# Output tiles of 128 columns and stores of 256, 128 and 126 rows in an FFT filter with a gated feed-forward block

## The chip, the core and the metric

The kernel runs on one core of a Trainium2 chip. TensorE (PE in the profile) multiplies matrices; its weight loads are listed apart as PEld. VectorE (DVE), ScalarE (ACT) and GpSimd (POOL) do the elementwise work. SyncE (SP) issues almost all DMAs, one after the other, from one queue of instructions; the transfers themselves run on 16 DMA engines that all queues of the core share. The metric is the device time of one execution in microseconds (us), and it is compared with the median of several executions.

## The reference

The input `x` has 8 sequences of 3136 tokens with 256 channels. Each channel is filtered in the frequency domain, and the result goes through a gated feed-forward block:

```python
X = np.fft.rfft(x, axis=1)
y = np.fft.irfft(X * (filt_r + 1j * filt_i)[None], n=x.shape[1], axis=1)

h = np.maximum(y @ w_in, 0.0)                       # 256 -> 1024
hp = pad(h, one zero token on either side)
conv_out = sum(conv_w[k] * hp[:, k:k + S, :] for k in range(3))
return (h / (1 + np.exp(-conv_out)) @ w_out)        # 1024 -> 256
```

The output has the shape of the input, 8 x 3136 x 256 in fp32, that is 25.7 MB.

## The kernel before

The Fourier transform is written as matrix products in four stages, each over 14 pairs of columns (`NP = 14`) of one sequence: stage 1 multiplies `x` with a table and stores to `a_dram`; stage 2 loads from `a_dram`, multiplies with a small table and applies the filter on DVE and POOL; stage 3 multiplies with a table and stores to `b_dram`; stage 4 loads from `b_dram` and leaves the filtered sequence in SBUF as two fp32r halves, `yh` and `yl` (a high part and the rest, so that products are made as three matmuls each). The first sequence is transformed ahead of the main loop. The transforms of the other seven are spread over the main loop: stages 2, 3 and 4 are 98 pieces there and stage 1 is 94, since four of them are done ahead of the loop. A stage-1, stage-2 or stage-3 piece is 2 to 4 matmul records (`L231`, `L235`) on a PSUM bank `ps_t`, a stage-4 piece is 8 (`L255`). A stage can start only when all 14 pieces of the stage before are stored.

The feed-forward block treats the eight sequences as one line of 25,095 positions (one zero token between two of them) and cuts it in 50 units of `UO = 510` positions. A unit needs eight steps, one for each block of 128 hidden channels, which makes 400 steps; the last eight, of unit 49, have only 105 positions. Step `m` is written out in this order (the order in the program is the order on each engine, a manual schedule): `evacuate` of the step seven back, the second half of the transform pieces of step `m - 1` (`from_bank`: a store to `a_dram` or `b_dram`, or the filter), new loads, the first half of the pieces of step `m` (`transform`), then `inner` (6 matmuls of 512 columns into a PSUM bank `ps_h`), `relu` and `centre` (ACT), the taps of the convolution (DVE), `sigmoid` (ACT), `gate` (DVE), `round_g` (ACT, the high half of the gated values), `rest_g` (POOL, the low half), and `project` of the step six back. Each batch of transforms is planned over 48 steps, which are six units.

`project` multiplies the gated values with `w_out`. The gated values `g` (128 hidden channels x 510 positions) are the stationary operand, cut in four tiles of 128, 128, 127 and 127 columns; each tile takes three matmuls of 256 columns. Two tiles share one of two PSUM banks, so the first bank `po0` holds 256 output rows and the second, `po1`, holds 254. After the last of the eight steps `evacuate` copies each bank to an SBUF tile `ot` (DVE, `L522`) and SP stores it: one DMA of 256 rows, written as 2 x 128 partitions, and one of 254 rows, written as 2 x 127 partitions (`L527`); a row is 1 KB. Only where a zero token falls into a bank is it stored in up to two pieces for each tile (`L533`, `L535`). Before unit 42 other DMAs follow these stores on SP: loads, tables, filters and stores of the transforms.

The values of the convolution (`t`) and the gated values (`g0`, `g1`) rotate through pools of four buffers each, 510 values, which is 2040 bytes in each partition.

DMAs issued by SP rotate over eight semaphores. Each waits first for the DMA that had the semaphore before it, and the queue behind it waits with it.

Of the kernel before, what the change touches and what calls it, by code (L numbers as in the profile page):

```python
# [9 lines left out]
F32 = mybir.dt.float32  # L10
F32R = mybir.dt.float32r
# [5 lines left out]
S = 3136  # L17
# [3 lines left out]
D = 256  # L21
# [3 lines left out]
UO = 510  # L25
ROW = S + 1
# [96 lines left out]
def tile_fft_filter_gated_ffn(  # L123
# [16 lines left out]
    nc = tc.nc  # L140
    B = x.shape[0]

    def hi_act(dst, src):
        nc.scalar.activation(dst, src, AF.Copy)  # L144
# [4 lines left out]
    def lo_pool(dst, src, hi):  # L149
        nc.gpsimd.tensor_tensor(out=dst, in0=src, in1=hi.bitcast(F32), op=ALU.subtract)  # L150
# [111 lines left out]
    with (  # L262
# [4 lines left out]
        raws, ws, fts, tabs, rows, zs, pss = {}, {}, {}, {}, {}, {}, {}  # L267
# [154 lines left out]
    wp = ctx.enter_context(tc.tile_pool(name="wp", bufs=2, reuse_waits="tile"))  # L422
# [4 lines left out]
    outf = out.rearrange("b s d -> (b s) d")  # L427
    LEN = B * ROW - 1
    NU = -(-LEN // UO)
    ts, hs, gs, pos, joined = {}, {}, {}, {}, {}  # L430

    def at(m):

        return (m // NF, m % NF) if 0 <= m < NF * NU else None

    def place(u):

        b, tok = divmod(UO * u, ROW)
        return b, tok, min(UO, LEN - UO * u)
# [30 lines left out]

    def centre(u, f):
        n = place(u)[2]
        ts[u, f] = t = wp.tile([128, UO], F32, name="t", bufs=4)[:, 0:n]
        nc.scalar.activation(t, hs[u, f][:, 1:n + 1], AF.Copy, scale=cw[:, 1, f:f + 1])  # L474

    def tap(u, f, k):
# [7 lines left out]
        nc.vector.tensor_mul(ts[u, f], hs.pop((u, f))[:, 1:place(u)[2] + 1], ts[u, f])  # L484

    def round_g(u, f):
        gs[u, f] = [wp.tile([128, UO], F32R, name=f"g{h}", bufs=4)[:, 0:place(u)[2]] for h in range(2)]
        hi_act(gs[u, f][0], ts[u, f])

    def rest_g(u, f):  # L490
        lo_pool(gs[u, f][1], ts.pop((u, f)), gs[u, f][0])

    def tiles_of(u):

        n = place(u)[2]
        if n <= 128:
            return [(0, n)]
        assert n == UO
        return [(0, 128), (128, 128), (256, 127), (383, 127)]

    def project(u, f):
        gh, gl = gs.pop((u, f))
        if f == 0:
            pos[u] = [ps_o.tile([128, 512], F32, name=f"po{k}") for k in range(2)]
        for t, (c, n) in enumerate(tiles_of(u)):
            o = pos[u][t // 2][0:n, t % 2 * D:t % 2 * D + D]
            first, last = f == 0 and t % 2 == 0, f == NF - 1
            nc.tensor.matmul(o, lhsT=gh[:, c:c + n], rhs=wo[0][:, f], start=first, stop=False, skip_group_check=True)  # L508
            nc.tensor.matmul(o, lhsT=gh[:, c:c + n], rhs=wo[1][:, f], start=False, stop=False, skip_group_check=True)  # L509
            nc.tensor.matmul(o, lhsT=gl[:, c:c + n], rhs=wo[0][:, f], start=False, stop=last, skip_group_check=True)  # L510

    def evacuate(u, f):
        if f < NF - 1:
            return
        tiles = tiles_of(u)
        for k in range(2):
            part = tiles[2 * k:2 * k + 2]
            if not part:
                continue
            n = part[0][1]  # L520
            ot = wp.tile([128, 2, D], F32, name="ot", bufs=3)[0:n, 0:len(part)]
            nc.vector.tensor_copy(ot.rearrange("p t d -> p (t d)"), pos[u][k][0:n, 0:len(part) * D])  # L522
            p = UO * u + part[0][0]
            b, tok = divmod(p, ROW)
            if tok + len(part) * n <= S:
                rows = outf[p - b:p - b + len(part) * n].rearrange("(t p) d -> p t d", p=n)
                nc.sync.dma_start(out=rows, in_=ot)  # L527
                continue
            for t in range(len(part)):
                b, tok = divmod(p + t * n, ROW)  # L530
                r, end = p + t * n - b, min(n, S - tok)
                if end > 0:
                    nc.sync.dma_start(out=outf[r:r + end], in_=ot[0:end, t])  # L533
                if end + 1 < n:
                    nc.sync.dma_start(out=outf[r + end:r + n - 1], in_=ot[end + 1:n, t])  # L535

    NW = 6 * NF
    plan, tails, heads = {}, {}, {}
# [102 lines left out]
    with tc.manual_schedule(engines=COMPUTE | {mybir.EngineType.SP}):  # L641
# [4 lines left out]
        for m in range(NF * NU + PLAG + 1):  # L646
            p1, p2, p3, p4, p6, p7 = (at(m - k) for k in (1, 2, 3, 4, PLAG, PLAG + 1))
            new, old = plan.get(m, []), plan.get(m - 1, [])
            if p7:
                evacuate(*p7)  # L650
# [11 lines left out]
            if p1:  # L662
                relu(*p1)
                centre(*p1)
# [4 lines left out]
            if p3:  # L669
                round_g(*p3)  # L670
# [3 lines left out]
            if p4:  # L674
                rest_g(*p4)
# [49 lines left out]
```

## Time and profile before

| | us |
|---|---|
| median of three runs | 1828.39 |
| lowest and highest | 1823.7 and 1836.49 |
| the profiled execution | 1834.37 |
| its span, first to last instruction | 1832.4 |
| DVE, ACT, POOL busy | 1182.3, 1151.3, 817.0 |
| first matmul of the main loop | 119.7 |

The profile has one row for each group of instructions: the line of the kernel, the engine, the operation, the tile written and those read. Records of matmuls overlap, as they are pipelined: 0.28 us in a row of the timeline is not the pace, which is the distance of two starts. The chain of work that ended last goes back from the last instruction to what released it; its rows have a start, a length and the instruction or the transfer, and are lengths along the chain. In the timeline of SP a row is a DMA instruction and its length is the time that SP's sequencer needed to issue it; the transfer comes after it. The table of stretches lists for each stretch its length, the busy time of the engines asked for with the number of instructions, the granted clock of TensorE, the mean share of the 16 DMA engines that is busy, and GB/s.

### The profile page before, as it was taken

What the parts mean: (1) busy time and instruction counts of PE and PEld (TensorE: products, weight loads), DVE (VectorE), ACT (ScalarE), POOL (GpSimd) and SP (SyncE); (2) the same over time, 40 slices, a digit from 0 to 9 for tenths busy, and PEclk for the clock granted to TensorE, in tenths of its full rate; (3) what the DMA queues carried; (4) which work ended last, traced back from release to release, by engine and by line L of the source; (5) the groups of instructions that cost most, each with busy time, mean ns of one, the idle gap of its engine ahead of it and who ended that gap; (6) DMA issues with size and microseconds to landing.
All of it is one profiled execution on the core that took longest, in us unless ns stands there. A gap on an engine that the chain in (4) does not pass through costs nothing.

```text
span 1832.4 us, 26781 instructions
## 1 busy us (share of the span) xinstructions
PE 1625.3 (89%) x9384; PEld 1402.4 (77%) x9384; DVE 1182.3 (65%) x1810; ACT 1151.3 (63%) x1989; POOL 817.0 (45%) x695
## 2 busy tenths in 40 slices
PE   6889879888898888988889899897998799999997
PEld 5778668777787677877778677886878678989997
DVE  6757655566655665666666667665765578767775
ACT  3376456655676556755478555774666656778885
POOL 3514435433453334634346334553445444564443
PEclk8899899999999999999999999998999899999999
DMA  9635543354524545245542464326542254310000
GB/s 273 200 111 175 184 145 104 117 166 139 160 69 123 162 138 159 65 129 158 161 141 71 132 207 144 107 67 183 177 139 85 66 158 140 109 35 25 25 24 28
DMA packets 159016, 229.16 MB, mean 125 GB/s; under 512 B 14970, under 2 KB 108002, under 8 KB 158882
## 3 DMA queue, kind: packets, MB, share of 16 engines
q1 hardware_dynamic: 157922, 226.53, 41.0%
q8 instruction: 75, 1.23, 0.3%
q10 hardware_dynamic: 960, 0.92, 0.2%
q14 instruction: 59, 0.48, 0.1%
HBM read 156.74 MB, written 70.65 MB: 124 GB/s over the span
## 4 chain that ended last, share of the span: by engine, by line
PE 60%; DMA 20%; issue 9%; POOL 4%; ACT 4%; DVE 2%; SPq 1%; POOLq 0%; ACTq 0%; DVEq 0%
PE ps_h L175 8%; PE ps_h L176 8%; PE ps_h L177 8%; DMA tin<-b_dram 7%; PE po L508 7%; PE po L509 7%; PE po L510 7%; PE ps_t L231 7%; DMA a_dram<-st 5%; PE ps_t L255 4%; PE ps_t L235 4%; POOL g L150 3%; DMA tab<-in_s 2%; DMA tab<-in_i 1%; DMA tin<-a_dram 1%
## 5 line engine op out<-in xcount | busy, mean ns | idle before, releaser
L478 DVE SCALAR_TENSOR_TENSOR t<-ps_h,cw,t 128x510 f32<-128x510 f32 (+1 forms) x800 | 588.5, 736 | 420.9 <-ACT t L474 418.1
L150 POOL TENSOR_TENSOR g<-t,g 128x510 fp32r<-128x510 f32 (+1 forms) x400 | 503.9, 1268 | 238.3 <-ACT g L144 215.1
L469 ACT ACTIVATE ps_h<-ps_h 128x512 f32<-128x512 f32 (+1 forms) x400 | 233.0, 583 | 364.6 <-PE ps_h L177 364.4
L508 PE MATMUL po<-wo,g 128*128 128x256 f32 (+2 forms) x1576 | 451.7, 287 | 0.7 <-DVE ot L522 0.5
L509 PE MATMUL po<-wo,g 128*128 128x256 f32 (+2 forms) x1576 | 450.1, 286 | 0.0
L510 PE MATMUL po<-wo,g 128*128 128x256 f32 (+2 forms) x1576 | 445.8, 283 | 0.0
L247 POOL TENSOR_TENSOR z<-z,v 120x512 f32<-120x512 f32 x112 | 147.3, 1315 | 552.6 <-DVE v L246 405.1
L474 ACT ACTIVATE t<-ps_h,cw 128x510 f32<-128x510 f32 (+1 forms) x400 | 272.3, 681 | 130.0 <-POOL g L150 96.1
L175 PE MATMUL ps_h<-y,wi 128*128 128x512 f32 (+1 forms) x688 | 338.5, 492 | 0.0
L508 PEld LDWEIGHTS po<-wo,g 128*128 128x128 f32 (+2 forms) x1576 | 304.1, 193 | 19.9 <-ACT t L474 1.5
L509 PEld LDWEIGHTS po<-wo,g 128*128 128x128 f32 (+2 forms) x1576 | 303.2, 192 | 17.9
L510 PEld LDWEIGHTS po<-wo,g 128*128 128x128 f32 (+2 forms) x1576 | 303.4, 192 | 0.6 <-POOL g L150 0.5
L176 PE MATMUL ps_h<-y,wi 128*128 128x512 f32 (+1 forms) x688 | 278.6, 405 | 0.3 <-DVE y L147 0.3
L177 PE MATMUL ps_h<-y,wi 128*128 128x512 f32 (+1 forms) x688 | 278.7, 405 | 0.0
L484 DVE TENSOR_TENSOR t<-ps_h,t 128x510 f32<-128x510 f32 (+1 forms) x400 | 268.5, 671 | 0.9 <-ACT t L481 0.8
L144 ACT ACTIVATE g<-t 128x510 fp32r<-128x510 f32 (+1 forms) x400 | 245.2, 613 | 4.4 <-PE po L509 4.0
L481 ACT ACTIVATE t<-t 128x510 f32<-128x510 f32 (+1 forms) x400 | 245.4, 613 | 2.1 <-DVE t L478 2.0
L150 POOL TENSOR_TENSOR y<-z,y 128x448 fp32r<-128x448 f32 x98 | 136.8, 1404 | 171.6 <-ACT y L144 171.6
L226 ACT ACTIVATE st<-ps_t 112x512 f32<-112x512 f32 x192 | 113.5, 594 | 98.6 <-DMA b_dram<-st 63.6
L175 PEld LDWEIGHTS ps_h<-y,wi 128*128 128x128 f32 x688 | 136.0, 198 | 39.0 <-issue 18.0
L176 PEld LDWEIGHTS ps_h<-y,wi 128*128 128x128 f32 x688 | 136.4, 198 | 38.0 <-issue 18.6
L177 PEld LDWEIGHTS ps_h<-y,wi 128*128 128x128 f32 x688 | 135.0, 196 | 31.8
(80 smaller groups left out, 1713.6 us busy)
## 6 DMA issues: line engine op xcount, KB each, us to landing
filt<-in_filt SPq DMA_DIRECT2D x98, 512.0 KB
tin<-a_dram SPq DMA_DIRECT2D x98, 224.0 KB
b_dram<-st SPq DMA_DIRECT2D x98, 224.0 KB
tin<-b_dram SPq DMA_DIRECT2D x98, 224.0 KB
tin<-in_x SPq DMA_DIRECT2D x94, 224.0 KB
a_dram<-st SPq DMA_DIRECT2D x94, 224.0 KB
out<-ot SPq DMA_DIRECT2D x46, 254.0 KB
out<-ot SPq DMA_DIRECT2D x45, 256.0 KB
```

The source lines that it names most:

```text
L144: nc.scalar.activation(dst, src, AF.Copy)
L150: nc.gpsimd.tensor_tensor(out=dst, in0=src, in1=hi.bitcast(F32), op=ALU.subtract)
L175: nc.tensor.matmul(ps, lhsT=wh, rhs=rh, start=start, stop=False, **kw)
L176: nc.tensor.matmul(ps, lhsT=wh, rhs=rl, start=False, stop=False, **kw)
L177: nc.tensor.matmul(ps, lhsT=wl, rhs=rh, start=False, stop=stop, **kw)
L474: nc.scalar.activation(t, hs[u, f][:, 1:n + 1], AF.Copy, scale=cw[:, 1, f:f + 1])
L478: nc.vector.scalar_tensor_tensor(out=t, in0=h[:, k:place(u)[2] + k], scalar=cw[:, k, f:f + 1], in1=t, op0=ALU.mult, op1=ALU.add)
L481: nc.scalar.activation(ts[u, f], ts[u, f], AF.Sigmoid)
L484: nc.vector.tensor_mul(ts[u, f], hs.pop((u, f))[:, 1:place(u)[2] + 1], ts[u, f])
L508: nc.tensor.matmul(o, lhsT=gh[:, c:c + n], rhs=wo[0][:, f], start=first, stop=False, skip_group_check=True)
L509: nc.tensor.matmul(o, lhsT=gh[:, c:c + n], rhs=wo[1][:, f], start=False, stop=False, skip_group_check=True)
L510: nc.tensor.matmul(o, lhsT=gl[:, c:c + n], rhs=wo[0][:, f], start=False, stop=last, skip_group_check=True)
```

## The change

Three things change. The second bank of a unit is made of tiles of 128 columns too, the last of which reads two columns past the 510 positions; they are set to zero once and never written again, and the two output rows that they give are not stored. The second bank is stored by a DMA of 128 rows and one of 126. And the gated values lie in four fixed pairs of tiles, `ring`, used in turn by `f % 4`; these and the tiles `t` are 576 values long, 2304 bytes, of which 510 are used.

```diff
+    ring = [[wp.tile([128, UO + 66], F32R, name=f"g{i}{h}", bufs=1) for h in range(2)] for i in range(4)]
+    for pair_of in ring:
+        for g in pair_of:
+            nc.gpsimd.memset(g[:, UO:UO + 2].bitcast(F32), 0.0)
...
-        ts[u, f] = t = wp.tile([128, UO], F32, name="t", bufs=4)[:, 0:n]
+        ts[u, f] = t = wp.tile([128, UO + 66], F32, name="t", bufs=4)[:, 0:n]
...
-        gs[u, f] = [wp.tile([128, UO], F32R, name=f"g{h}", bufs=4)[:, 0:place(u)[2]] for h in range(2)]
-        hi_act(gs[u, f][0], ts[u, f])
+        gs[u, f] = ring[f % 4]
+        hi_act(gs[u, f][0][:, 0:place(u)[2]], ts[u, f])
...
-        return [(0, 128), (128, 128), (256, 127), (383, 127)]
+        return [(0, 128), (128, 128), (256, 128), (384, 128)]
...
-            if tok + len(part) * n <= S:
-                rows = outf[p - b:p - b + len(part) * n].rearrange("(t p) d -> p t d", p=n)
+            if k == 0 and len(part) == 2 and tok + 256 <= S:
+                rows = outf[first - b:first - b + 256].rearrange("(t p) d -> p t d", p=128)
                 nc.sync.dma_start(out=rows, in_=ot)
                 continue
-            for t in range(len(part)):
-                b, tok = divmod(p + t * n, ROW)
-                r, end = p + t * n - b, min(n, S - tok)
-                if end > 0:
-                    nc.sync.dma_start(out=outf[r:r + end], in_=ot[0:end, t])
-                if end + 1 < n:
-                    nc.sync.dma_start(out=outf[r + end:r + n - 1], in_=ot[end + 1:n, t])
+            for t, (c, n) in enumerate(part):
+                i, n = 0, min(n, place(u)[2] - c)
+                while i < n:
+                    b, tok = divmod(UO * u + c + i, ROW)
+                    if tok == S:
+                        i += 1
+                        continue
+                    end = min(n, i + S - tok)
+                    if end - i > 16 and (end - i) % 14:
+                        end = i + (end - i) // 16 * 16
+                    r = b * S + tok
+                    nc.sync.dma_start(out=outf[r:r + end - i], in_=ot[i:end, t])
+                    i = end
```

Pieces of the output that are neither of 16 rows or fewer nor a multiple of 14 are cut to a multiple of 16, and the rest follows as a piece of its own.

On the engines this shows at two places. SP's queue at unit 0, within the first batch of transforms, before; a name is the target of the DMA and what it reads, with the shape on the SBUF side, and the numbered DMAHW in brackets is the semaphore whose last DMA is waited for:

```order
133 L590 DMA tab<-in_s 112x224 [waits DMAHW2_49]
134 L527 DMA out<-ot 128x2x256 [waits DMAHW3_49,DVE_49]
135 L527 DMA out<-ot 127x2x256 [waits DMAHW4_49,DVE_49]
136 L227 DMA a_dram_59<-st 112x2x256 [waits DMAHW5_49,Activation_49]
137 L221 DMA tin<-a_dram_58 112x512 [waits DMAHW6_49,PE_49]
```

and now:

```order
133 L601 DMA tab<-in_s 112x224 [waits DMAHW2_49]
134 L532 DMA out<-ot 128x2x256 [waits DMAHW3_49,DVE_49]
135 L545 DMA out<-ot 128x256 [waits DMAHW4_49,DVE_49]
136 L545 DMA out<-ot 126x256 [waits DMAHW5_49]
137 L227 DMA a_dram_59<-st 112x2x256 [waits DMAHW6_49,Activation_49]
138 L221 DMA tin<-a_dram_58 112x512 [waits DMAHW7_49,PE_49]
```

The store of 2 x 127 partitions has become two stores, and everything behind it takes the next semaphore in turn; nothing has changed places.

The end of SP's queue, units 47, 48 and 49, before:

```order
821 L527 DMA out<-ot 128x2x256
822 L527 DMA out<-ot 127x2x256
823 L527 DMA out<-ot 128x2x256
824 L527 DMA out<-ot 127x2x256
825 L527 DMA out<-ot 105x256
```

and now:

```order
873 L532 DMA out<-ot 128x2x256
874 L545 DMA out<-ot 128x256
875 L545 DMA out<-ot 126x256
876 L532 DMA out<-ot 128x2x256
877 L545 DMA out<-ot 128x256
878 L545 DMA out<-ot 126x256
879 L545 DMA out<-ot 96x256
880 L545 DMA out<-ot 9x256
```

The last unit's 105 rows go as 96 and 9. In all SP issues 170 stores of the output where it issued 113. PE, DVE and ACT issue the same instructions in the same order as before, with 128 in the place of 127; POOL has eight small memsets more, ahead of the first step's work.

## What was predicted

> **What bounds the kernel now.** I read the page first, then the chain of waits, then SP's timeline, and last tables of stretches and the waits of PE.
>
> ```profile
> span 1832.4 us, 26781 instructions
> PE 1625.3 (89%) x9384; PEld 1402.4 (77%) x9384; DVE 1182.3 (65%) x1810; ACT 1151.3 (63%) x1989; POOL 817.0 (45%) x695
> ...
> PE 60%; DMA 20%; issue 9%; POOL 4%; ACT 4%; DVE 2%; SPq 1%; POOLq 0%; ACTq 0%; DVEq 0%
> ```
>
> PE is busy for 89%, but only 60% of the chain is PE and 20% is transfers. The full list of the chain shows which: among its longest pieces are 14 loads or stores of the transforms that take 13.5 to 14.5 us each; these are the first and the last.
>
> ```profile
> 298.10 14.31 DMA tin<-b_dram
> ...
> 1607.40 14.21 DMA tin<-b_dram
> ```
>
> SP's timeline shows what stands ahead of them. Two units of one batch:
>
> ```profile
> 558.12 0.99 SPq L527 DMA_DIRECT2D out<-ot  x2
> 559.20 8.21 SPq L227 DMA_DIRECT2D a_dram<-st  x1
> 573.29 0.79 SPq L221 DMA_DIRECT2D tin<-a_dram  x2
> ...
> 595.90 8.14 SPq L227 DMA_DIRECT2D b_dram<-st  x1
> ```
>
> A DMA is issued in 0.3 to 0.5 us, but the one behind a pair of output stores takes 8.2 us, and SP issues nothing meanwhile. Which store does it shows in the table of stretches after the last transform, where the stores of a unit (issued at 1642) are alone (the columns are the length of the stretch, granted clock, DMA share, GB/s):
>
> ```profile
> 1642.00:1644.00 2.00, 1.00 0.40 132
> 1644.00:1646.00 2.00, 1.00 0.06 7
> ...
> 1650.00:1654.00 4.00, 1.00 0.07 24
> ```
>
> After 2 us of spread traffic (the 256 rows) a share of 0.06 to 0.07 stays for ten more: 1 of 16 engines. So the store of 2 x 127 partitions runs on a single DMA engine; what is issued behind it needs that engine too, lands after some 14 us, and is held 8 us in its issue. PE pays for it. One batch of six units, and a stretch after the transforms:
>
> ```profile
> 571.00:796.00 225.00, 198.63 (x1119) 170.62 (x1118) 139.36 (x212) 137.89 (x236) 99.20 (x83) 0.93 0.44 132
> 1640.00:1665.00 25.00, 24.88 (x159) 22.18 (x159) 20.73 (x33) 21.10 (x37) 12.86 (x11) 1.00 0.10 32
> ```
>
> The columns are PE, PEld, DVE, ACT, POOL, granted clock, DMA share, GB/s. In the batch PE is idle for 26.4 us and its clock is 0.93; afterwards it is 99.5% busy at 1.00 and sets the pace. The idle time of PE in that batch, by what ended it:
>
> ```profile
> PE ps_t L255 <- DMA tin<-b_dram: 7.1, 2, 4.4
> PE ps_t L231 <- DMA tab<-in_s: 6.1, 1, 6.1
> PE ps_t L235 <- DMA tin<-a_dram: 5.1, 1, 5.1
> PE ps_t L235 <- issue: 5.0, 1, 5.0
> PE ps_t L231 <- issue: 1.1, 1, 1.1
> PE ps_t L231 <- DMA tab<-in_i: 0.9, 1, 0.9
> PE ps_t L231 <- ACT st L226: 0.7, 1, 0.7
> PE ps_t L255 <- PE ps_t L255: 0.5, 1, 0.5
> ```
>
> The first four, 23.3 us, are loads that were issued behind a blocked SP or ran on the loaded engine; 3.2 us are small.
>
> **What PE needs without these waits.** I price the work at full clock from the chain, where a row ends as the next begins.
>
> ```profile
> 617.31 0.86 PE ps_t L235 x2
> 618.17 0.23 PE ps_h L175
> ...
> 620.99 1.08 PE ps_t L231 x5
> ...
> 629.23 0.86 PE ps_t L231 x4
> ...
> 1627.24 0.88 PE ps_t L255 x8
> ```
>
> A step without transforms is 620.99 - 618.17 = 2.82 us. A piece of stage 2 (`L235`) is 0.86, of stage 1 or 3 (`L231`) 0.86, of stage 4 (`L255`) 0.88. So: 392 steps x 2.82 = 1105.4; stages 1 to 3, (94 + 98 + 98) x 0.86 = 249.4; stage 4, 98 x 0.88 = 86.2. Ahead of the main loop lie 119.7 us (its first matmul), behind the last full step, from 1803.8, 28.6 us:
>
> ```profile
> L175 PE MATMUL ps_h<-y,wi x688: 213/399/1415, 119.7 to 1817.7; 128*128 128x512 f32 x168, 128*128 128x108 f32 x4
> ...
> 1803.67 0.28 PE L510 MATMUL po<-wo,g 128*127 128x256 f32 x1
> 1816.59 9.33 SPq L527 DMA_DIRECT2D out<-ot  x3
> ```
>
> The sum is 1589.3 us, 243 less than the span. That 243 is idle PE and PE at the lower clock after each pause; a batch by the same prices is 48 x 2.82 + 14 x 3.46 = 183.8 us, against 225 measured.
>
> **The change part by part.**
>
> *Stores of 256, 128 and 126 rows.* The 46 stores of 254 rows go. The 128 rows are the first store's form cut in half. For 126 no row shows the spread; bounds: as good as 128 rows (nothing held), or one engine as 127 rows were where a zero token forced them alone:
>
> ```profile
> 1085.92 0.25 SPq L533 DMA_DIRECT2D out<-ot  x1
> 1086.27 2.24 SPq L227 DMA_DIRECT2D a_dram<-st  x1
> ```
>
> There the next issue took 2.24 us, not 8.2. I take the first: the rows show 2 x 128 partitions spread and 2 x 127 not, 127 is a prime, and 126 can be dealt out evenly, as 9 rows for each of 14 engines. "DMA: Bandwidth & Descriptors" of the Trainium skill (section "Why a DMA increments its semaphore by 16 and not by 1") says that a transfer uses the largest number of engines up to 16 that divides its slowest dimension, so 127 gives 1 and 126 gives 14. By that rule the first bound holds; the share of 0.06 agrees with the 1, and no row here shows the 14.
>
> With nothing held, the loads have time: a stage's first load is issued at least two steps of 3 us or more ahead of its use, and the 2 us that the 256 rows took above are the scale of a spread transfer. So the 23.3 us per batch go, and the slow clock behind them, as PE then has no pause longer than 1 us. What is late next are the 3.2 us of small waits: 6.5 batches x 3.2 = 21 us if all stay, 0 if they too came from SP; between ends that near I take the middle, +10.
>
> *57 more issues on SP* (170 stores, not 113), 0.25 to 0.5 us each, 23 us over the run, ahead of the loads in SP's queue. For the copies to `ot` alone SP waits far longer, and with the loads running several pieces ahead this is hidden; I cost it at nothing.
>
> ```profile
> SPq L527 <- DVE ot L522: 338.2, 79, 24.7
> ```
>
> If that cover were gone, 23 us is the end. The semaphores in turn are taken up one place earlier; since no DMA then stays out for 14 us, their waits shrink.
>
> Here a rule speaks against the change. "SBUF — State Buffer" of the Trainium skill (section "The DMA setup-cost knee") gives every transfer a fixed cost of about 2 us and asks for one large transfer, not several. By it 57 more would be an estimated 114 us if nothing hid them, and the sum 1707 us; the trace disagrees for this kernel, whose one large transfer is the one that blocks.
>
> *The end.* The last store of 105 rows is issued behind a 254-row store: three issues, with their waits, take 9.33 us from 1816.59 to 1825.9, and the landing lasts to the end at 1832.4, 6.5 us more. Behind spread stores the landing is some 2 us, like the 256 rows above, which is -4.5, and part of the issue is hold: -6 us, with 0 and -8 as ends.
>
> *128 columns for 127.* The loads of weights on PE by shape:
>
> ```profile
> L508 PEld LDWEIGHTS po<-wo,g 128*128 128x128 f32 x784 | 153.6, 196 | 19.6 <-ACT t L474 1.5
> ...
> L508 PEld LDWEIGHTS po<-wo,g 128*127 128x127 f32 x784 | 149.1, 190 | 0.0
> ```
>
> A load is 6 ns longer, but overlaps its neighbours, and the matmul streams 256 columns either way: 0. Bounds: 2352 x 6 ns = +14 us if it lies on the path, and as much below if mixed widths cost something now. The copies to `ot` have one more partition, no more elements in each: 0.
>
> *Fixed tiles, 2304 bytes apart.* The same four-deep turn, and the same waits on PE, DVE and ACT; eight memsets on POOL are under 1 us, hidden by the first steps. Whether the distance changes a pace no row shows; 0, with the 14 us above as its bound either way.
>
> **Sum.** 1589.3 - 6 + 10 = 1593 us of span. The profiled execution has 2.0 us around its span (1834.4) and is 0.33% above the median of the runs, 1828.4; so 1595 x 0.9967 = 1590 us.
>
> **The rivals.**
>
> *126 rows run on one engine too, so the change does half of what it says.* By the row above a quarter of the hold stays (2.24 for 8.2), by the bytes half of the transfer (126 of 254 KB). The gain of 243 - 6 shrinks by a quarter to a half, 59 to 118 us; some 1680. For it: no row shows 126. Against: 127 is the one odd number here.
>
> *ACT becomes the bound in stage 4.* With PE's pauses gone nothing lets ACT catch up.
>
> ```profile
> L474 ACT ACTIVATE t<-ps_h,cw 128x510 f32<-128x510 f32 x392 | 269.5, 687 | 129.2 <-POOL g L150 96.1 <-ACT ps_h L469 1.1
> L481 ACT ACTIVATE t<-t 128x510 f32<-128x510 f32 x392 | 243.1, 620 | 1.6 <-DVE t L478 1.6
> L144 ACT ACTIVATE g<-t 128x510 fp32r<-128x510 f32 x392 | 242.9, 620 | 2.2 <-PE po L509 1.9
> L469 ACT ACTIVATE ps_h<-ps_h 128x512 f32<-128x512 f32 x392 | 231.0, 589 | 362.8 <-PE ps_h L177 362.6
> ...
> L144 ACT ACTIVATE y<-z 128x448 fp32r<-128x448 f32 x98 | 102.0, 1075 | 1.7 <-DVE z L630 1.7
> ```
>
> A step with one stage-4 piece is 3.59 us on ACT and 2.82 + 0.88 = 3.70 on PE. If gaps between ACT's instructions and the stores of stage 1 make it 4.0, 98 steps lose 0.3 each: +30 us, 1620. Over a whole batch ACT's 137.9 us are well under 183.8, so it is a loss of that stage alone.
>
> *SP's issues are on the path after all*, so that every further transfer costs its 0.4 us: 57 x 0.4 = +23, 1613. For it: the queue is in order, and loads stand behind the stores. Against: the 338 us above.
>
> *Slower.* The 4704 matmuls of `project` read their weights from tiles at another distance, and PE is the bound: if that or the full width stretched each by 52 ns, the gain of 243 is lost. The nearest row is the 6 ns above, so I see no reason for so much.
>
> **How the numbers follow.** Chances: my forecast, within 1565 to 1615, 0.73; ACT, 1610 to 1650, 0.11; SP's issues, 1605 to 1650, 0.04; 126 rows on one engine, 1650 to 1710, 0.06; below 1565, where widths and small waits all fall my way, 0.03; no gain or a loss by PE's weights, 0.03. The predicted time is the first's, 1590. The range from 1562 to 1650 holds the first three and leaves out about 0.12. A measurement of this kernel can tell about 1% from no change: faster by more 0.97, within 0.01, slower 0.02.
>
> **What would show it.** In the new profile: no DMA issue of 8 us behind the stores; no 14 us piece in the chain; DMA's part of the chain below 10%; a batch of six units in 184 to 190 us, PE over 95% busy, clock 0.98 or more; steps after the transforms still 2.8 us, which tests width and distance. I am wrong if an issue behind the 126 rows still takes 2 us or more, if PE waits for ACT through stage 4, or if steps at the end differ from 2.8 us.

## The result, and the profile after

| | before | after |
|---|---|---|
| median of four runs each, us | 1827.35 | 1588.72 |
| lowest and highest of the changed kernel, us | | 1583.21 and 1590.12 |
| ratio of the times, 95% interval | | 0.868, 0.864 to 0.872 |
| span of the profiled execution, us | 1832.4 | 1581.2 |
| mean granted clock | 0.943 | 0.991 |

The changed kernel takes 13.2% less time. One execution of the kernel before, run beside the three experiments that hold SP longer, spread the stores in time and use four engines, took 5295 us and is left out of their ratios. The page of its profile, the lines on busy time and on the shares of the chain:

```profile
span 1581.2 us, 26837 instructions
PE 1532.2 (97%) x9384; PEld 1334.5 (84%) x9384; DVE 1180.3 (75%) x1810; ACT 1150.4 (73%) x1989; POOL 821.7 (52%) x703
...
PE 87%; DMA 3%; issue 3%; ACT 2%; DVE 2%; POOL 1%; SPq 0%; ACTq 0%; POOLq 0%; DVEq 0%
```

PE, DVE, ACT and POOL do the same work as before (but for the eight memsets), in a span 251 us shorter. PE's own busy time fell by 93 us, 12 to 18 of them by the width (below) and most of the rest, as it seems, by the higher clock; the other 158 us were idle. Transfers fell from 20% of the chain to 3%. What is left of them shows in the list of the longest pieces of the chain (start, length, what):

```profile
33.76 8.43 DMA tab<-in_i
42.25 4.50 DMA f<-in_filt
62.69 8.43 DMA f<-in_filt
...
128.08 4.28 DMA tab<-in_s
```

All but the last lie ahead of the main loop, which begins at 118.4 us; no transfer of 14 us is left. SP's timeline around the stores of one unit shows why (start, time that the issue took, instruction):

```profile
579.47 0.41 SPq L532 DMA_DIRECT2D out<-ot  x1
580.30 0.83 SPq L545 DMA_DIRECT2D out<-ot  x2
581.23 0.34 SPq L227 DMA_DIRECT2D b_dram<-st  x1
581.67 0.37 SPq L221 DMA_DIRECT2D tin<-in_x  x1
```

The issues of the three stores take 1.2 us, and that of the DMA behind them 0.34 us, where it took 8.2 us. Whether the 126 rows are spread is read after the transforms, where a unit's stores are alone. The table of stretches (length, busy time of PE, clock, DMA share, GB/s), from the first store of a unit at 1422.27:

```profile
1422.00:1424.00 2.00, 2.00 (x13) 1.00 0.40 137
1424.00:1426.00 2.00, 2.00 (x15) 1.00 0.40 124
1426.00:1430.00 4.00, 4.00 (x30) 1.00 0.00 0
```

Before, a share of 0.06 to 0.07 followed the first 0.40 and stayed for ten microseconds; now 0.40 stays until all is stored, and then there is nothing. In the records of completions, a store of 126 rows has 15 (one comes 0.6 us after the issue, 14 with the data), and one of 127 rows has 2.

The batches of transforms, in stretches of 185 us and one after the transforms (length; PE, PEld, DVE, ACT, POOL; clock, DMA share, GB/s):

```profile
330.00:515.00 185.00, 182.94 (x1118) 158.50 (x1116) 137.82 (x211) 137.14 (x234) 99.79 (x83) 1.00 0.53 158
515.00:700.00 185.00, 183.52 (x1119) 158.93 (x1118) 139.24 (x214) 138.12 (x236) 99.82 (x83) 1.00 0.54 160
700.00:885.00 185.00, 182.63 (x1119) 158.12 (x1118) 139.57 (x213) 138.26 (x237) 100.09 (x83) 1.00 0.54 161
1400.00:1560.00 160.00, 159.82 (x1039) 144.35 (x1038) 126.60 (x191) 133.73 (x232) 75.76 (x59) 1.00 0.09 27
```

PE is idle for 1.5 to 2.4 us in 185, and its clock is full. Measured from step to step, six whole batches take 184.0 to 187.3 us (218 to 225 before).

### The profile page after: what moved, and what is told of

Its sections match the earlier page's. It is cut to its first block, busy times and chain, and to the rows that moved or that the text cites. A ratio compares the mean times of both kernels' runs of the same rounds, so it can differ in the third digit from the quotient of the medians.

```text
span 1581.2 us, 26837 instructions
## 1 busy us (share of the span) xinstructions
PE 1532.2 (97%) x9384; PEld 1334.5 (84%) x9384; DVE 1180.3 (75%) x1810; ACT 1150.4 (73%) x1989; POOL 821.7 (52%) x703
## 4 chain that ended last, share of the span: by engine, by line
PE 87%; DMA 3%; issue 3%; ACT 2%; DVE 2%; POOL 1%; SPq 0%; ACTq 0%; POOLq 0%; DVEq 0%
PE ps_h L175 11%; PE ps_h L176 11%; PE ps_h L177 11%; PE po L514 11%; PE po L515 11%; PE po L516 11%; PE ps_t L231 10%; PE ps_t L255 6%; PE ps_t L235 5%; DMA rows<-in_x 1%; DMA f<-in_filt 1%; POOL g L150 1%; DMA tab<-in_i 1%; ACT y L144 0%; ACT br L327 0%
## 5 line engine op out<-in xcount | busy, mean ns | idle before, releaser
L514 PE MATMUL po<-wo,g 128*128 128x256 f32 (+1 forms) x1576 | 439.3, 279 | 0.2 <-DVE ot L527 0.2
L515 PE MATMUL po<-wo,g 128*128 128x256 f32 (+1 forms) x1576 | 438.3, 278 | 0.0
L516 PE MATMUL po<-wo,g 128*128 128x256 f32 (+1 forms) x1576 | 438.0, 278 | 0.0
L175 PE MATMUL ps_h<-y,wi 128*128 128x512 f32 (+1 forms) x688 | 325.3, 473 | 0.0
L514 PEld LDWEIGHTS po<-wo,g 128*128 128x128 f32 (+1 forms) x1576 | 296.6, 188 | 17.8 <-ACT t L478 0.6
L515 PEld LDWEIGHTS po<-wo,g 128*128 128x128 f32 (+1 forms) x1576 | 296.2, 188 | 16.6
L516 PEld LDWEIGHTS po<-wo,g 128*128 128x128 f32 (+1 forms) x1576 | 296.4, 188 | 0.6 <-POOL g L150 0.5
L176 PE MATMUL ps_h<-y,wi 128*128 128x512 f32 (+1 forms) x688 | 269.4, 392 | 0.2 <-DVE y L147 0.2
L177 PE MATMUL ps_h<-y,wi 128*128 128x512 f32 (+1 forms) x688 | 269.0, 391 | 0.0
L175 PEld LDWEIGHTS ps_h<-y,wi 128*128 128x128 f32 x688 | 129.9, 189 | 35.9 <-issue 16.6
L176 PEld LDWEIGHTS ps_h<-y,wi 128*128 128x128 f32 x688 | 130.4, 190 | 34.4 <-issue 16.7
L177 PEld LDWEIGHTS ps_h<-y,wi 128*128 128x128 f32 x688 | 129.6, 188 | 29.8
L226 ACT ACTIVATE st<-ps_t 112x512 f32<-112x512 f32 x192 | 113.2, 591 | 10.9 <-PE ps_t L231 10.9
```

What stands on the lines that cost most here:

```text
L175: nc.tensor.matmul(ps, lhsT=wh, rhs=rh, start=start, stop=False, **kw)
L176: nc.tensor.matmul(ps, lhsT=wh, rhs=rl, start=False, stop=False, **kw)
L177: nc.tensor.matmul(ps, lhsT=wl, rhs=rh, start=False, stop=stop, **kw)
```

## The experiments

Four theories were on the table. *Standstill*: the store of 254 rows on one DMA engine hurts because SP's queue stands behind it. *Load*: it hurts because that engine is busy and loads have their share on it. *Width*: tiles of 127 columns cost PE something themselves. *Distance*: so does the distance of 2040 or 2048 bytes between tiles. Each kernel is compared with the kernel before in runs on the same chip, so ratios are compared where kernels ran on different ones. The edits shown are against the changed kernel.

### Which of the three parts brings it

**The stores alone.** The kernel before, with its widths and its tiles, and the new code for the stores; the second bank of a unit goes as 112 and 15 rows, twice.

```diff
-    ring = [[wp.tile([128, UO + 66], F32R, name=f"g{i}{h}", bufs=1) for h in range(2)] for i in range(4)]
...
-        gs[u, f] = ring[f % 4]
+        gs[u, f] = [wp.tile([128, UO], F32R, name=f"g{h}", bufs=4)[:, 0:place(u)[2]] for h in range(2)]
...
-        return [(0, 128), (128, 128), (256, 128), (384, 128)]
+        return [(0, 128), (128, 128), (256, 127), (383, 127)]
```

> The kernel before with one part of the change: the output is stored in the new pieces. The tiles keep their widths of 128, 128, 127 and 127 columns, so the second bank goes as 112 and 15 rows twice; the pools of t and g and their distance of 2040 bytes stay. If the one-engine store is the whole gain, the time is that of the changed kernel, 1589 us, ratio to before 0.87. If the width or the distance of the tiles gives the shorter steps at the end (2.74 to 2.81 us after, 2.79 to 2.85 before), it is 400 steps x 0.035 us = 14 us longer, 1603, ratio 0.877, and the steps at the end are 2.79 to 2.85 us again. If tiles gave a large part of the gain, the time is over 1650 us.

1601.97 us, ratio 0.875 (0.874 to 0.877). The stores alone bring 228.5 us of the gain. The changed kernel, run again beside it, took 1586.1, so some 16 us belong to the other two parts.

**The width put back.** Everything of the change but the 128 columns.

```diff
-        return [(0, 128), (128, 128), (256, 128), (384, 128)]
+        return [(0, 128), (128, 128), (256, 127), (383, 127)]
```

> The changed kernel with tiles of 128, 128, 127 and 127 columns; the fixed tiles 2304 bytes apart stay; the second bank goes as 112 and 15 rows twice. If the width sets the shorter steps, the time is 1603 us and the starts of the third tile's matmuls are 123 and 132 ns apart again. If the distance sets them, the time is 1589 us and all starts are 113 to 114 ns apart. If it is partly the one and partly the other, it lies between, with the third tile slow and the others at 113.

1600.98 us, ratio 0.875 (0.874 to 0.877): the same as the stores alone, so fixed tiles and their distance bring nothing at this width.

**The distance put back.** 2048 bytes for 2304, for the gated values and for `t`.

```diff
-    ring = [[wp.tile([128, UO + 66], F32R, name=f"g{i}{h}", bufs=1) for h in range(2)] for i in range(4)]
+    ring = [[wp.tile([128, UO + 2], F32R, name=f"g{i}{h}", bufs=1) for h in range(2)] for i in range(4)]
...
-        ts[u, f] = t = wp.tile([128, UO + 66], F32, name="t", bufs=4)[:, 0:n]
+        ts[u, f] = t = wp.tile([128, UO + 2], F32, name="t", bufs=4)[:, 0:n]
```

> The changed kernel with the tiles t and g 512 values long, 2048 bytes apart, not 2304; widths of 128 and the new stores stay. If the width sets the shorter steps, 1589 us and steps of 2.74 to 2.81 us at the end. If the distance of 2304 bytes does, 1603 us and 2.79 to 2.85. Any larger loss would mean that tiles 2048 bytes apart get in each other's way on ACT, DVE or POOL, whose instructions of 510 values would then be longer than 582, 679 and 1285 ns.

1586.19 us, ratio 0.866 (0.865 to 0.868).

**The changed kernel again**, on the same chip.

> The changed kernel once more on the same chip as the three before it, as the measure for differences below one per cent: 1589 us, ratio 0.868 to 0.870 by every theory.

1586.14 us, ratio 0.867 (0.864 to 0.869). The distance is worth nothing, and the width 1600.98 - 1586.14 = 15 us: five runs from 1599.4 to 1602.7 against four from 1581.0 to 1590.1. How PE shows it: the same stretch after the transforms, 130 us in which PE has no pause, of the kernel with the width put back,

```profile
1430.00:1560.00 130.00, 130.00 (x832) 1.00 0.08 25
```

and of the one with the distance put back:

```profile
1430.00:1560.00 130.00, 130.00 (x847) 1.00 0.08 25
```

With clock and busy time equal, 1.8% more matmuls fit into it. Where they gain is seen in the timeline of PE. The first three matmuls with a 127-column tile and the one after them, width put back:

```profile
1505.03 0.29 PE L514 MATMUL po<-wo,g 128*127 128x256 f32 x1
1505.15 0.29 PE L515 MATMUL po<-wo,g 128*127 128x256 f32 x1
1505.28 0.28 PE L516 MATMUL po<-wo,g 128*127 128x256 f32 x1
1505.40 0.28 PE L514 MATMUL po<-wo,g 128*127 128x256 f32 x1
```

and the third tile's three and their successor at 128 columns, distance put back:

```profile
1504.41 0.28 PE L514 MATMUL po<-wo,g 128*128 128x256 f32 x1
1504.53 0.28 PE L515 MATMUL po<-wo,g 128*128 128x256 f32 x1
1504.64 0.28 PE L516 MATMUL po<-wo,g 128*128 128x256 f32 x1
1504.75 0.28 PE L514 MATMUL po<-wo,g 128*128 128x256 f32 x1
```

From start to start it is 0.12, 0.13 and 0.12 us, against 0.12, 0.11 and 0.11. The last digit is coarse, so here are the means over some 46 steps after the transforms: the first two matmuls of the third tile take 122.6 and 131.1 ns at 127 columns and 113.2 and 113.2 at 128, and a step 2814 and 2769 ns. The six matmuls of `inner` are 231 to 233 ns apart in both. (With the width put back the stores also go in 96 pieces more. An experiment below prices 95 more at 0.3%, some 5 us with a larger uncertainty; PE's pace doesn't hang on it.)

### Why the one store cost so much

**Second bank on one engine, in halves.** 127 and 113 rows, each of which falls to one engine, and the 1 and 13 rows that are left. The bytes on that engine are nearly those of the kernel before (240 for 254 rows), in two transfers.

```diff
-                    if end - i > 16 and (end - i) % 14:
+                    if end - i in (126, 128) and k == 1:
+                        end = i + {128: 127, 126: 113}[end - i]
+                    elif end - i > 16 and (end - i) % 14:
```

> The changed kernel, but the second bank of a unit is stored as 127 and 1 and as 113 and 13 rows: 240 of its 254 rows go in two transfers whose partition counts are primes, so on one engine each. If the one-engine store is the cause, most of the gain goes: the engine is taken 240/254 of the time, the issue behind the pair is held about 7 us (before 8.2), and the time is 1589 + 0.9 x 240 = about 1800 us. If a tile's width or distance were the cause, it stays below 1620 us.

1774.22 us, ratio 0.971 (0.962 to 0.980). 188 us of the gain are gone, with the width and the tiles of the change untouched. SP's timeline at the same unit:

```profile
579.32 0.41 SPq L532 DMA_DIRECT2D out<-ot  x1
580.00 7.52 SPq L547 DMA_DIRECT2D out<-ot  x4
587.62 0.32 SPq L227 DMA_DIRECT2D b_dram<-st  x1
```

The issues are held again, for 7.5 us over four stores. In the whole loop 84 issues took over 1.5 us, 296 us in all (before: 43 and 315; after: 9 and 16).

**On two engines.** 122 rows for 127 and for 113; 122 is 2 x 61, and these stores have three completions, one early and two with data.

```diff
+                        end = i + {128: 122, 126: 122}[end - i]
```

> The changed kernel with 122 and 6 and with 122 and 4 rows: 122 = 2 x 61, so two engines if the number of engines is the largest number up to 16 that divides the partitions. 244 rows on two engines are 122 on each, as long as one 127-row store on one engine, behind which the next issue took 2.2 us: the hold falls to about 2 us and landings to 7 us. Theory: half to three quarters of the loss is gone, 1630 to 1700 us. If only a single engine were harmful, 1589.

1608.51 us, ratio 0.880 (0.873 to 0.888): a miss, the loss is 1.4% of the time before, less than was expected. The transfers still take 4.3 to 8.3 us, but only 13 issues are held over 1.5 us, 23 us in all. The loss follows the hold, not the length of the transfer.

**SP held, no engine loaded.** The stores of the change, and behind a unit's last one four DMAs of 4 KB, each of which reads what the one ahead wrote, so that SP waits for each. It stands for 5.6 us in the mean, of which 4 are waits and the rest the issues between them.

```diff
+    small = wp.tile([16, 64], F32, name="small", bufs=1)
+    scratch = dram.tile([16, 64], F32, name="scratch")
...
+            if k == 1:
+                for _ in range(2):
+                    nc.sync.dma_start(out=small, in_=scratch)
+                    nc.sync.dma_start(out=scratch, in_=small)
```

> The changed kernel with good stores, and after each unit's stores four tiny DMAs of 16 x 256 bytes on SP, each waiting for the one before it, so SP's queue stands still for about 4 x 1.9 = 7 to 8 us while no engine is loaded. If the hold of SP's queue is what costs, the time goes most of the way back, 1750 to 1800 us. If the loaded engine is (what is issued behind the store lands late), the loss is small, below 1640 us.

1648.17 us, ratio 0.902 (0.895 to 0.909), between the two expectations: the standstill costs something by itself, but at some 6 us little. So its length was doubled.

**SP held longer.** Eight such DMAs (`range(4)`), 11.3 us in the mean.

> The changed kernel with good stores and eight tiny dependent DMAs behind each unit's stores instead of four, so SP's queue stands still for about 8 x 1.5 = 12 us, 6 us more than in e7, and no engine is loaded. Before the change the loads behind a pair of stores landed 14 us after it, 11 us late. Theory that SP's standstill is the cause, and that the loads run some 6 us ahead: e7's 6 us cost 62 us, and each us beyond that costs a us in each of 42 units, so 1648 + 42 x 4 to 6 = 1810 to 1900 us, as slow as before the change or slower. Theory that the loaded engine is needed for the loss: below 1720 us.

1899.47 us, ratio 1.035 (1.028 to 1.043): slower than before and at the upper end of the first expectation, though the large stores run on 14 or 16 engines as in the changed kernel. The waits of SP, and then those of PE in 245 us of it (what waited for what; us in total, times, longest):

```profile
SPq L555 <- DMA small<-scratch: 249.3, 196, 3.7
...
SPq L554 <- DMA scratch<-small: 152.3, 147, 2.8
```

```profile
PE ps_t L255 <- DMA tin<-b_dram: 8.6, 2, 6.2
PE ps_t L231 <- DMA tab<-in_s: 6.2, 1, 6.2
PE ps_t L235 <- DMA tin<-a_dram: 5.7, 1, 5.7
```

SP waited 402 us for the small DMAs in 49 places, and PE lacks the same loads as in the kernel before. In the kernel held half as long it waited 198 us (142.5 and 55.1 in the same rows). Twice the standstill cost almost five times as much (3.6% and 16.9% more than the changed kernel, in ratios to the kernel before): a stop of some 6 us is mostly covered, as it seems by loads that are already in flight, and one of some 12 us isn't.

**The one-engine stores from ACT's queue.** The halves of 127 and 113 rows, issued by ACT behind its rounding; the small stores and all loads stay on SP. If only the held issue did the harm, it would be gone from SP.

```diff
+                    if k == 1 and end - i in (127, 113):
+                        late.append((outf[r:r + end - i], ot[i:end, t]))
+                    else:
+                        nc.sync.dma_start(out=outf[r:r + end - i], in_=ot[i:end, t])
...
+            for dst, src in late:
+                nc.scalar.dma_start(out=dst, in_=src)
```

> The stores of e5 with the two one-engine pieces issued from ACT's queue, after ACT's rounding in the same step: SP is not held, while the one engine is as loaded as in e5. If the hold of SP's queue costs, the time is near the changed kernel's, 1600 to 1630 us, the 20 us for two issues per unit on ACT. If the loaded engine costs, 1700 us or more, and the transfers of SP land up to 14 us after their issue as before.

1758.13 us, ratio 0.962 (0.955 to 0.970): hardly better than on SP's queue. By itself this would speak for the loaded engine. But the other sign of it is missing: SP's loads and stores of the transforms land 8.0 us after the start of their issue at the latest, not 14 (8.4 in the changed kernel). And SP stands here too. Its timeline behind one unit's stores, and then its waits:

```profile
571.91 0.86 SPq L552 DMA_DIRECT2D out<-ot  x2
572.87 0.32 SPq L227 DMA_DIRECT2D b_dram<-st  x1
573.28 0.38 SPq L221 DMA_DIRECT2D tin<-in_x  x1
573.71 1.09 SPq L608 DMA_DIRECT2D tab<-in_s  x1
574.89 0.39 SPq L608 DMA_DIRECT2D tab<-in_i  x1
582.51 0.31 SPq L227 DMA_DIRECT2D b_dram<-st  x1
582.91 0.38 SPq L227 DMA_DIRECT2D a_dram<-st  x1
588.54 0.30 SPq L221 DMA_DIRECT2D tin<-a_dram  x1
```

```profile
SPq L221 <- DMA out<-ot: 206.7, 39, 7.4
...
SPq L227 <- DMA out<-ot: 87.4, 17, 8.0
...
SPq L613 <- DMA out<-ot: 57.5, 11, 7.0
...
SPq L608 <- DMA out<-ot: 27.0, 9, 5.7
```

Each of the eight semaphores is used again eight DMAs later, whichever engine issues it. The 127 rows issued at 571.91 landed at 582.44, and SP, whose next DMA needed their semaphore, went on at 582.51; the 113 rows landed at 588.48, and SP went on at 588.54. In these four rows SP waited 379 us for stores of the output. The held issue was gone from SP, and its place was taken by a wait at the semaphore. ACT was held instead: those of its issues that took over 1.5 us add up to 66 us, and PE's waits for ACT's copies to `st` rose from 3.6 to 15.8 us. So this run doesn't tell of SP alone.

**The same bytes on one engine, spread in time.** 248 of the 254 rows of the second bank as eight stores of 31 rows (31 is a prime: two completions, one with data), one in each of the next eight steps.

```diff
+                    if k == 1 and end - i in (126, 128):
+                        r = b * S + tok
+                        for j in range(4):
+                            late.append((outf[r + 31 * j:r + 31 * j + 31], ot[i + 31 * j:i + 31 * j + 31, t]))
...
+            if late:
+                dst, src = late.pop(0)
+                nc.sync.dma_start(out=dst, in_=src)
```

> The changed kernel, but 248 of the second bank's 254 rows go in eight stores of 31 rows, a prime, so on one engine each, and one of them is issued in each of the unit's eight steps. The one engine carries as many bytes for each unit as before, in eight pieces of about 1.7 us instead of one of 14. Theory that a long standstill of SP behind one long transfer is the cause: 1590 to 1615 us. Theory that the load of the one engine, with the share of all others that it carries too, is the cause: over 1700 us.

1592.42 us, ratio 0.868 (0.864 to 0.872): the gain stays whole. The table of issues shows the bytes, and a stretch after the transforms, where the queue isn't in use otherwise, that one engine carries them:

```profile
out<-ot SPq DMA_DIRECT2D x380, 31.0 KB
```

```profile
1426.00:1428.00 2.00, 2.00 (x13) 1.00 0.06 15
1428.00:1430.00 2.00, 2.00 (x15) 1.00 0.07 24
```

380 x 31 KB is 11.8 MB, as the 46 x 254 KB of the kernel before. The load on the engine, spread in time, does no harm by itself; neither do 380 more DMAs in SP's queue.

**On four engines.** 124 rows (4 x 31) for 127 and 113.

> The changed kernel with 124 and 4 and with 124 and 2 rows: 124 = 4 x 31, so four engines each. 248 rows on four engines are 62 on each, 3.4 us; no issue is held and no transfer lands later than the loads can bear. 1587 to 1595 us, the changed kernel's time within one per cent; two engines gave 1608.

1595.59 us, ratio 0.870 (0.865 to 0.874); the transfers land in 2.8 to 6.0 us, and 3 issues took over 1.5 us.

All of it in a table. Its columns are the sum of the issues that took over 1.5 us in the main loop (for ACT's queue 5 us on SP and 66 on ACT), the waits of SP for stores of the output (at their semaphores), and its waits for the small DMAs, in us. The loss is the difference of the ratios to that of the changed kernel, 0.8665 (for the kernel before to 0.875, as it has the other width); the ratios are known to 0.2 to 0.9%, so the first three rows can't be told apart:

| stores of the second bank | held issues | semaphores | small DMAs | loss |
|---|---|---|---|---|
| 128 and 126 rows, 16 and 14 engines | 16 | 1 | | 0 |
| eight of 31 rows, one engine, spread in time | 10 | 22 | | 0.1% |
| 124 rows, four engines | 5 | 3 | | 0.3% |
| 122 rows, two engines | 23 | 42 | | 1.4% |
| as after, SP made to wait some 6 us | 7 | 1 | 198 | 3.6% |
| 127 and 113 rows, one engine, ACT's queue | 71 | 385 | | 9.6% |
| 127 and 113 rows, one engine | 296 | 58 | | 10.5% |
| 254 rows, one engine (before) | 315 | 57 | | 12.5% |
| as after, SP made to wait some 12 us | 7 | 1 | 402 | 16.9% |

The loss goes with the time that SP stands, however it is brought to stand. PE shows it too: its idle time after 150 us is 16, 15, 22, 31, 55, 125, 140, 167 and 230 us in the order of the rows. The larger losses exceed what the idle time grew by, and the granted clock fell with them (0.99 in the first row, 0.93 in the last). Only the kernel with ACT's queue costs less than its sum would say; there the stop of a unit comes in two pieces, which may be why, but no run tests it. *Load* alone falls where it is spread in time, by the row of 31 rows; *standstill* alone is enough, by the last row.

One question is left: how much of the loss before is the held issue, and how much the late landing of what was issued behind it on the same engine, up to 14 us after the issue began. The records of completions answer most of it. Of the 14.0 us of the DMA whose issue began at 559.20, 8.2 are its own held issue, and from the end of the issue it landed after 5.8 us. In the changed kernel SP's loads and stores of the transforms take 3.1 us for that in the median and 7.9 at most. So the late landing is the hold and some 3 us more. Landing some 1 us later costs nothing here: with the stores of 31 rows the median is 4.1 us, as in the kernel before (4.2), at a loss of 0.1%. What the 3 us cost behind one long transfer no run shows by itself.

## Why the prediction came out

*The stores.* Its main step held: 23.3 us per batch of long waits, and the slow clock behind them, went with the 254-row stores. PE's idle time after 150 us fell from 167.4 to 16.3 us. The prediction put the waits down to loads that "were issued behind a blocked SP or ran on the loaded engine"; the runs show the first to be enough. What the prediction didn't see is that a stop is not in proportion to what it costs: 6 us cost a fifth of what 12 us do.

*126 rows.* Taken as spread, and they are: 0.40 of the engines while they move, 14 completions with data, 0.34 us in the median for the issue behind. The rule that the prediction cited from "DMA: Bandwidth & Descriptors" of the Trainium skill (section "Why a DMA increments its semaphore by 16 and not by 1") agrees in all six sizes tried: 126 on 14, 124 on 4, 122 on 2, and 127, 113 and 31 rows on 1. The rival of 1680 us falls. Its price, 59 to 118 us for one half on one engine, stays untested: the kernel with both halves there lost 188 us.

*57 more issues, 0.* Right: 95 DMAs more than in the changed kernel (1026 for 931 in the main loop) came at 0.3% with four engines, and 380 more at 0.1% with the stores of 31 rows. The estimate of 1707 us, which rests on the fixed cost of some 2 us in the section "The DMA setup-cost knee" of "SBUF — State Buffer" of the Trainium skill, was given for the case that nothing hides that cost. It is hidden here: a 126-row store lands 2.1 us after its issue in the median, and SP waits 1.5 us in all for stores of the output.

*Small waits, +10.* 16.3 us of idle time after 150 us, inside its ends of 0 and 21. *The end, -6.* From the last full step to the end 20.7 us, for 28.6: -8, at the edge of what was given.

*128 columns for 127, 0.* This is the term that was mis-sized. It compared the mean length of a load of weights (190 and 196 ns) and found that the wider one is 6 ns longer and hidden. What counts is the distance of the matmuls' starts, and that is smaller with 128 columns: 45 ns a step over 392 steps are 18 us of the span, 15 us in the comparison of the kernels, just beyond the bound of -14. The prediction's own test for it, a step after the transforms still at 2.8 us, fails when it is read closely: 2.77 for 2.82. The right row to ask was in the trace of before: the starts of consecutive matmuls by tile show 122.7 and 131.0 ns for the first two of the third tile and 114 to 118 in all others.

*Fixed tiles and 2304 bytes, 0.* Right: 1586.19 and 1586.14.

*The sum.* By its own terms with the measured sizes: 1589.3 - 1 (the loop begins 1.3 us earlier) - 18 (width) - 8 + 16 = 1578 us of span, against 1581.2 and, in the second set, 1588.0 in the profiled executions. The forecast of 1593 us of span was high by the width, low by 6 us of small waits, and the rest is within what the executions of one kernel differ by. The median came out at 1589 for 1590; so close a hit is partly luck, as the width's 18 us that the sum left out were made up for by the small waits and by differences that no term has.

*The other rivals.* ACT does not become the bound: in 185 us PE waits 0.7 us for it,

```profile
PE ps_t L231 <- ACT st L226: 0.7, 1, 0.7
PE ps_t L255 <- PE ps_t L255: 0.5, 1, 0.5
PE ps_t L231 <- PE ps_t L231: 0.2, 1, 0.2
```

and these three are all of PE's waits in the stretch from 515 to 700 us. SP's issues are not on the path, as told. The loss by PE's weights is refuted in sign: the matmuls that use them got faster.

## What to carry to other kernels

A store whose rows can't be dealt out evenly to several engines (127 here) is to be looked for before anything else in the queue: its cost is not its own length but the time for which the in-order queue behind it stands, and cutting it in other pieces was worth 12.5% here, while moving it to another issuing queue moved the stop, on SP, to the next use of its semaphore and held the other queue as well. Ask how far ahead the loads run (here some 6 us, as the two lengths of stop suggest): a stop of about that length cost 3.6%, and one of twice that length 16.9%. And when PE is the bound, read the pace from the starts of consecutive matmuls, by tile, before calling an odd tile width free.

## What the runs showed of the hardware

- Tiles of 127 columns slow the stream of matmuls: in the first odd tile two matmuls take 122.6 and 131.1 ns for 113.2, in the second odd one they take 115 to 118 for 113 to 114, and the last one of 128 columns ahead of them takes 117.8 for 113.7. Yet a load of 127 columns of weights is shorter than one of 128 (190 and 196 ns in the mean in the kernel before). Nothing here shows why.
- An issue is held for long where many rows go to one engine: behind 254 rows 8.2 us, behind 127 rows alone 1.7 to 2.2 us, behind two engines with 61 rows each 0.5 us in the median, though the transfers of the last took up to 8.3 us. It isn't the only case: in the changed kernel nine issues took 1.5 to 2.3 us, seven of them loads and stores of the transforms.
- Two engines lost 1.4% against fourteen, four 0.3%, which is within the noise.
- In this program a DMA issued from ACT's queue is tied to SP's by the semaphore that both use in turn: 385 us of waits for stores of the output, where the kernel before had 57.
- The tiles' distance, 2048 or 2304 bytes, changes no pace: 2769 and 2770 ns a step.
